# Attention ahead of two gated layers: the score, transpose and value stages one step further apart, and another order for the first steps

## The chip, the cores and the metric

The kernel runs on one core of one Trainium2 chip. The time is device microseconds for one execution of the whole program. Engines are named as the profile names them: PE (matrix multiply; PEld is its weight load), DVE (vector), ACT (scalar activation), POOL (GpSimd) and SP, which here only issues DMAs.

## The reference

Windowed causal attention feeds two dense layers in a row. All arrays are float32.

```
q, k, v: (4, 8, 576, 64)
scores = (q @ k^T) / 8 + slope_h * -|i - j|,  kept where 0 <= i - j < 128, else -1e9
attn   = softmax(scores) ;  a = attn @ v
x  = a as (2304, 512)                                  # tokens x (heads * 64)
x2 = (sigmoid(x @ w_gate) * (x @ w_val)) @ w_out        # 512 -> 1536 -> 512
h  = ((x2 @ w1) * (x2 @ w2)) @ w3                       # 512 -> 1024 -> 1024
out = h @ w_out2                                        # 1024 -> 512
```

## The kernel before

**Tiling.** The 2304 tokens are 18 tiles of 128, taken as five blocks of 2, 4, 4, 4 and 4 tiles (`TILES`). The 8 heads are four pairs; a pair fills 128 partitions. Attention is therefore 5 x 4 = 20 steps, step n being block n // 4 and pair n % 4 (`where`, `NSTEP`). The hidden width of the two layers is cut into slices of 128 that are taken two at a time (`groups`, `GF` = 2); a dense product is done in three float32r passes (high x high, high x low, low x high, `PASSES`), so every weight and every activation exists as a high and a low part.

**The three stages of an attention step.** `stage_s` (L418): PE computes the scores of up to four tiles and two heads into a PSUM tile that has a single buffer (`spsum`, tag `s`). For each two tiles DVE merges the two diagonals (L436), scales and adds the bias table (L439) and takes the negated row maximum (L445); for pairs other than the first ACT rescales that maximum (L449); ACT takes four exponentials with a row sum each (L452); DVE adds 1e-9 and inverts the sums (L455, L456); POOL multiplies each tile by its inverse (L459). `stage_p` (L461), for each of the two heads: PE transposes the tiles into a PSUM bank (L467), ACT copies it to `cp` (L470), POOL splits it by two selects into previous and own tile (L471, L475). `stage_pv` (L481): PE multiplies with v (L490), ACT and DVE write the high and low part of `xt` (L497, L498). Transposes, weighted values and the dense products below take their PSUM from one pool of four banks (`psmm`, tag `mm`).

**Fillers.** `layer(groups[0], blk)` is a generator for the first two slices of the first dense layer on one block: `gv` makes both gate products, then their sigmoids (ACT, L255), then the two value products, each followed by DVE's multiply (L260) and by the high and low parts `gt` (ACT, POOL); `down1` of the block before follows (L278). `fill(budget)` advances it by about that many ns of PE work. A layer for block b joins the list when the attention of that block is complete.

**The order.** PE's instructions run exactly in the order in which they are written (`manual_schedule`, L519). The other engines' and SP's order is laid down by a planner, which takes each instruction when it takes it to be ready, by priority; all queues are in order on the chip. Step n of the loop (L520) loads q and k for step n + 1 and v for step n + 1. For the first four steps it writes `stage_s(n)`, then `stage_p` and `stage_pv` of step n - 2; at step 4 scores, then both stages of steps 2 and 3, then the first filler; afterwards `stage_pv(n - 2)`, `stage_s(n)`, 600 ns of filler, `stage_p(n - 1)`, 3500 ns of filler.

**Weight conversion.** The weights arrive as float64 bit patterns. `convert_next` (L123) takes one from `queue`: ACT, five DVE instructions (L115 to L119) and POOL (L120) make a float32 (`rounded`), and ACT and POOL its two parts in `wsl`; or the float32 goes back to DRAM for a later stage. Twelve are taken during attention, at a priority 300 instructions later than their place: the six of the first group (`parts`, gate slices, then value slices, then output slices) and the six of the second, which are written to DRAM and fetched again once attention is over. The staging pool `conv0` is closed at step 15.

After attention the layers of all groups run over the blocks; nothing in the change touches that code.

Of the kernel before, what the change touches and what calls it, by code (L numbers as in the profile page):

```python
# [9 lines left out]
F32 = mybir.dt.float32  # L10
# [3 lines left out]
AF = mybir.ActivationFunctionType  # L14
ALU = mybir.AluOpType
# [4 lines left out]
P = 128  # L20

TILES = (2, 4, 4, 4, 4)
NBLK = len(TILES)
STARTS = tuple(sum(TILES[:i]) for i in range(NBLK))
TB = max(TILES) * P
# [4 lines left out]

PASSES = ((0, 0), (0, 1), (1, 0))
LATER = 300
FILL = (600.0, 3500.0)

FOLD_PLAN = ("cc", "ccccc", "cccfcfc", "cfcfcfcf", "cfcfcfcf")

# [8 lines left out]
def attn_moe_kernel(  # L45
# [14 lines left out]
    nc = tc.nc  # L60
# [77 lines left out]
    def convert_start(items):  # L138
        queue.extend(items)
        for it in queue[:2]:  # L140
            if it[0] not in staged:
                fetch(*it[:2])
# [10 lines left out]
            wsl[i] = wpools[par].tile([P, 3, 2, DM], F32R, name=f"wsl{i}", tag="w")  # L153
        return wsl[i][:, c, 0], wsl[i][:, c, 1]

    def parts(grp):
        def src(i, c):
            m = i - NF
            own = (w_gate, w_val, w_out)[c][i] if i < NF else (w1[m], w2[m], w3o[m * P : (m + 1) * P, :])[c]
            return ahead.get((i, c), own)  # L160

        return [((i, c), src(i, c), part_sink) for c in range(3) for i in grp]


    wo2 = {}
# [64 lines left out]
    def gv(grp, blk, xs, one):  # L230

        pss = {}
        w = cols(blk)
        ns = w / 2.4 + 13.3

        def product(i, s):
            full = gvpool.tile([P, TB], F32, tag=gvtag, name=f"gv{i}_{blk}_{s}", bufs=gvbufs)
            ps = pss[i, s] = full[:, 0:w]
            for kk in range(NK):
                for wp, xp in PASSES:  # L240
                    nc.tensor.matmul(  # L241
                        ps,
                        wsl[i][:, s, wp, kk * P : (kk + 1) * P],
                        xs[blk][:, xp, kk],
                        start=(kk == 0 and wp == 0 and xp == 0),
                        stop=(kk == NK - 1 and wp == 1),
                    )
                yield 3 * ns

        g = {}  # L250
        for i in grp:
            yield from product(i, 0)
        for i in grp:
            g[i] = m2.tile([P, TB], F32, tag="g", name=f"g{i}_{blk}")[:, 0:w]
            nc.scalar.activation(g[i], pss[i, 0], AF.Sigmoid if one else AF.Copy)  # L255
        ts = []
        for i in grp:
            yield from product(i, 1)
            pr = g[i]
            nc.vector.tensor_tensor(pr, pr, pss[i, 1], ALU.mult)  # L260
            t = m2.tile([P, 2, TB], F32R, tag="gt", name=f"gt{i}_{blk}", bufs=4)[:, :, 0:w]
            act_copy(t[:, 0], pr)
            pool_lo(t[:, 1], pr, t[:, 0])
            ts.append(t)
        return ts
# [61 lines left out]
    def attention(actx, conv):  # L327
# [9 lines left out]

        ident = cpool.tile([P, P], F32, name="ident")
        mask = cpool.tile([P, P], I32, name="mask")
        base = cpool.tile([P, 7, P], F32, name="base")  # L340

        PAIRS = {"nf": 0, "fn": 1, "nn": 2, "nc": 3, "ca": 4, "an": 5}
        KINDS = "fnnncannn" * 2
# [68 lines left out]

        def load_v(n):
            pair, blk, nt, t0, back = where(n)
            t = loads[n]["v"] = ap2.tile([P, 5, P], F32, tag="ldv", name=f"ldv{n}", bufs=4)
            nc.sync.dma_start(t[:, 1 - back : 1 + nt], v[pair, :, t0 - back : t0 + nt])

        def stage_s(n):  # L418
            pair, blk, nt, t0, back = where(n)
            s, ld = st[n], loads[n]  # L420
            x = s["sm"] = ap2.tile([P, 4, 2, P], F32, tag="sm", name=f"sm{n}", bufs=3)

            ps = spsum.tile([P, 4, 2, 2, P], F32, tag="s", name=f"s{n}")
            for t in range(nt):
                for h in range(2):
                    r = slice(D * h, D * h + D)
                    nc.tensor.matmul(  # L427
                        ps[:, t // 2 * 2 + h, :, t % 2], ld["q"][r, t * P : (t + 1) * P],
                        ld["k"][r, t * P : (t + 2) * P],
                        start=True, stop=True, skip_group_check=True,  # L430
                    )
            up = 4.0**pair
            for tp in range(nt // 2):
                g = slice(2 * tp, 2 * tp + 2)

                nc.vector.copy_predicated(  # L436
                    ps[:, g, 1], mask.unsqueeze(1).unsqueeze(1).broadcast_to([P, 2, 2, P]), ps[:, g, 0]
                )
                nc.vector.scalar_tensor_tensor(  # L439
                    x[:, g].rearrange("p g u k -> p g (u k)"), ps[:, g, 1].rearrange("p g u k -> p g (u k)"),  # L440
                    0.125 * up, tabs[blk][:, g].rearrange("p g u k -> p g (u k)"), ALU.mult, ALU.add,
                )
                mn = ap2.tile([P, 4], F32, tag="mn", name=f"mn{n}_{tp}", bufs=4)
                su = ap2.tile([P, 4], F32, tag="su", name=f"su{n}_{tp}", bufs=4)
                nc.vector.tensor_reduce(  # L445
                    mn, x[:, g].rearrange("p g u k -> p (g u) k"), axis=AX.X, op=ALU.max, negate=True
                )
                if pair:
                    nc.scalar.activation(mn, mn, AF.Copy, scale=1.0 / up)  # L449
                for j in range(4):  # L450
                    y = x[:, 2 * tp + j // 2, j % 2]
                    nc.scalar.activation(  # L452
                        y, y, AF.Exp, bias=mn[:, j : j + 1], scale=1.0 / up, accum_out=su[:, j : j + 1]
                    )
                nc.vector.tensor_scalar_add(su, su, 1e-9)  # L455
                nc.vector.reciprocal(su, su)  # L456
                for j in range(4):
                    y = x[:, 2 * tp + j // 2, j % 2]
                    nc.gpsimd.tensor_scalar(y, y, su[:, j : j + 1], 1.0, ALU.mult, ALU.mult)  # L459

        def stage_p(n):  # L461
            pair, blk, nt, t0, back = where(n)
            s = st[n]
            for h in range(2):
                ps = gvpool.tile([P, 4, P], F32, tag="mm", name=f"pt{n}_{h}")
                for t in range(nt):
                    nc.tensor.transpose(ps[:, t], s["sm"][:, t // 2 * 2 + h, t % 2], ident)  # L467
                cp = ap2.tile([P, 4, 2, P], F32, tag="cp", name=f"cp{n}_{h}")
                own, prev = cp[:, 0:nt, 1], cp[:, 0:nt, 0]
                act_copy(own, ps[:, 0:nt])  # L470
                nc.gpsimd.affine_select(  # L471
                    out=prev, in_=own, compare_op=ALU.is_gt, fill=0.0, base=0,
                    pattern=[[0, nt], [-1, P]], channel_multiplier=1,
                )
                nc.gpsimd.affine_select(  # L475
                    out=own, in_=own, compare_op=ALU.is_ge, fill=0.0, base=0,
                    pattern=[[0, nt], [1, P]], channel_multiplier=-1,
                )
                s["cp", h] = cp.rearrange("p t c k -> p (t c k)")
# [22 lines left out]
        def fill(budget):  # L502

            while fillers and budget > 0:
# [3 lines left out]
                else:  # L508
                    budget -= cost

        load(0)
        convert_start(parts(groups[0]) + second_items)
        load(1)
        load_v(0)
        consts()
        make_identity(nc, ident)
        table(0)
        HOT = NPAIR + 2
        with tc.manual_schedule(engines={mybir.EngineType.PE}):  # L519
            for n in range(NSTEP + 2):  # L520
                if 2 <= n + 1 < NSTEP:
                    load(n + 1)
                if 1 <= n + 1 < NSTEP:
                    load_v(n + 1)
                if n == 1:
                    consts2()
                if n % NPAIR == NPAIR - 2 and n // NPAIR + 1 < NBLK:
# [1 line left out]
                if n == 15:  # L529
# [2 lines left out]
                    accpools.append(  # L532
                        ctx.enter_context(tc.tile_pool(name="acc1", bufs=1, side="right", reuse_waits="tile"))
                    )
                if n < NPAIR:
                    stage_s(n)
                    if n >= 2:
                        stage_p(n - 2)
                        stage_pv(n - 2)
                elif n == NPAIR:  # L540
                    stage_s(n)
                    for m in (n - 2, n - 1):
                        stage_p(m)
                        stage_pv(m)
                    fillers.append(layer(groups[0], 0))
                    fill(FILL[1])
                else:
                    if n - 2 >= NPAIR:
                        stage_pv(n - 2)
                        if (n - 2) % NPAIR == NPAIR - 1 and (n - 2) // NPAIR < NBLK - 1:  # L550
                            fillers.append(layer(groups[0], (n - 2) // NPAIR))
                    if n < NSTEP:
                        stage_s(n)
                    fill(FILL[0])
                    if n - 1 < NSTEP:
                        stage_p(n - 1)
                    fill(FILL[1])
                if queue and (n < NPAIR + 2 or n % 2 == 0 or n > 9):
                    convert_next()
            while fillers:  # L560
                for _ in fillers.pop(0):
# [105 lines left out]
```

## Time and profile before

| | |
|---|---|
| Median of 3 runs | 977.85 us (977.38 to 977.97) |
| The profiled execution | 979.05 us; span 977.1 us |
| PE busy | 912.4 us (93%), 4528 matmuls |
| DVE, ACT, POOL busy | 581.1 us (59%), 338.6 us (35%), 329.0 us (34%) |
| Attention, by the PE order | scores from 4.2 us, last weighted values end at 235.9 us |
| Mean granted TensorE clock | 0.97 of 2.4 GHz |

The slices of the page show where PE is not busy and not at full clock (40 slices of 24.4 us):

```profile
PE   2487888989999899999999999999999999999998
DVE  6676565554698789689687247962862632431313
PEclk9686899899999999999999999999999999999999
```

Each digit is a tenth of a slice. The first ten slices are attention; in the other thirty PE is at nine nearly throughout.

### The profile page before, as it was taken

What the parts mean: (1) busy time and instruction counts of PE and PEld (TensorE: products, weight loads), DVE (VectorE), ACT (ScalarE), POOL (GpSimd) and SP (SyncE); (2) the same over time, 40 slices, a digit from 0 to 9 for tenths busy, and PEclk for the clock granted to TensorE, in tenths of its full rate; (3) what the DMA queues carried; (4) which work ended last, traced back from release to release, by engine and by line L of the source; (5) the groups of instructions that cost most, each with busy time, mean ns of one, the idle gap of its engine ahead of it and who ended that gap; (6) DMA issues with size and microseconds to landing.
All of it is one profiled execution on the core that took longest, in us unless ns stands there. A gap on an engine that the chain in (4) does not pass through costs nothing.

```text
span 977.1 us, 12272 instructions
## 1 busy us (share of the span) xinstructions
PE 912.4 (93%) x4528; PEld 744.3 (76%) x4528; DVE 581.1 (59%) x983; ACT 338.6 (35%) x784; POOL 329.0 (34%) x427
## 2 busy tenths in 40 slices
PE   2487888989999899999999999999999999999998
PEld 1264666667887788888888887888888888888887
DVE  6676565554698789689687247962862632431313
ACT  4364668474232242242232134343321311311110
POOL 5867565554332241231232111112431421421211
PEclk9686899899999999999999999999999999999999
DMA  5443332210433325114212022323330200000012
GB/s 168 158 151 127 111 93 84 76 39 27 147 108 118 108 74 160 58 67 157 68 65 97 1 76 92 113 78 108 107 98 1 85 24 1 21 1 1 33 54 107
DMA packets 32602, 79.68 MB, mean 82 GB/s; under 512 B 3616, under 2 KB 5664, under 8 KB 32544
## 3 DMA queue, kind: packets, MB, share of 16 engines
q1 hardware_dynamic: 32544, 78.92, 25.1%
q8 instruction: 35, 0.57, 0.3%
q14 instruction: 23, 0.19, 0.1%
HBM read 65.27 MB, written 13.63 MB: 81 GB/s over the span
## 4 chain that ended last, share of the span: by engine, by line
PE 78%; DVE 8%; ACT 6%; POOL 4%; DMA 3%; issue 1%; SPq 0%; ACTq 0%; DVEq 0%; POOLq 0%
PE gv L241 44%; PE dn L278 13%; PE o L302 10%; PE pv L490 4%; PE w3o L207 4%; ACT sm L452 2%; PE s L427 2%; POOL sm L459 1%; PE pt L467 1%; POOL cp L471 1%; ACT cp L68 1%; ACT L452 1%; POOL cp L475 1%; DMA raw_(0, 0)_94<-in_w_gate_dram 1%; ACT L255 1%
## 5 line engine op out<-in xcount | busy, mean ns | idle before, releaser
L241 PE MATMUL gv<-xt,wsl 128*128 128x512 f32 (+1 forms) x1440 | 310.0, 373 | 4.5 <-DVE g L260 3.2
L241 PEld LDWEIGHTS gv<-xt,wsl 128*128 128x128 f32 x1440 | 252.2, 191 | 53.2 <-DVE g L260 4.3
L74 POOL TENSOR_TENSOR gt<-g,gt 128x512 fp32r<-128x512 f32 (+1 forms) x100 | 120.0, 1203 | 422.0 <-ACT gt L68 421.8
L241 PE MATMUL gv<-x,wsl 128*128 128x512 f32 (+1 forms) x960 | 200.2, 368 | 0.0
L241 PEld LDWEIGHTS gv<-x,wsl 128*128 128x128 f32 x960 | 167.6, 189 | 30.1
L260 DVE TENSOR_TENSOR g<-g,gv 128x512 f32<-128x512 f32 (+1 forms) x100 | 62.6, 630 | 161.9 <-PE gv L241 161.9
L278 PE MATMUL dn<-gt,wsl 128*128 128x512 f32 (+1 forms) x720 | 153.6, 369 | 0.0
L278 PEld LDWEIGHTS dn<-gt,wsl 128*128 128x128 f32 x720 | 126.0, 189 | 23.0 <-issue 0.3
L68 ACT ACTIVATE gt<-g 128x512 fp32r<-128x512 f32 (+1 forms) x100 | 58.4, 587 | 143.9 <-DVE g L260 143.8
L255 ACT ACTIVATE g<-gv 128x512 f32<-128x512 f32 (+1 forms) x100 | 54.7, 549 | 152.5 <-PE gv L241 147.7
L302 PE MATMUL o<-wsl,gt 128*128 128x512 f32 x432 | 101.1, 389 | 0.0
L302 PEld LDWEIGHTS o<-wsl,gt 128*128 128x128 f32 x432 | 80.9, 188 | 16.6
L490 PE MATMUL pv<-cp,ldv 128*64 128x256 f32 (+1 forms) x352 | 57.1, 406 | 30.9 <-POOL cp L475 16.6
L490 PEld LDWEIGHTS pv<-cp,ldv 128*64 128x64 f32 x352 | 33.8, 160 | 54.6 <-POOL cp L475 24.8
L287 DVE TENSOR_TENSOR acc<-acc,dn 128x512 f32<-128x512 f32 (+1 forms) x100 | 62.3, 628 | 21.4 <-PE dn L278 20.9
L459 POOL TENSOR_SCALAR sm<-sm,su 128x128 f32<-128x128 f32 x144 | 56.4, 409 | 26.3 <-DVE su L456 19.2
L427 PE MATMUL s<-ldk,ldq 64*128 64x256 f32 x288 | 44.4, 453 | 16.3 <-DVE sm L439 6.2
L311 DVE TENSOR_TENSOR acc<-acc,o 128x512 f32<-128x512 f32 x54 | 37.1, 688 | 35.2 <-PE o L302 35.2
L452 ACT ACTIVATE sm<-sm,mn 128x128 f32<-128x128 f32 x144 | 55.9, 390 | 1.3 <-DVE mn L445 0.7
L427 PEld LDWEIGHTS s<-ldk,ldq 64*128 64x128 f32 x288 | 31.4, 224 | 25.0 <-issue 21.1
L207 PE MATMUL w3o<-wo,w3s 128*128 128x512 f32 x192 | 44.9, 391 | 0.7 <-DVE wo L71 0.5
L207 PEld LDWEIGHTS w3o<-wo,w3s 128*128 128x128 f32 x192 | 35.9, 188 | 9.1 <-DVE wo L71 0.8
(741 smaller groups left out, 861.7 us busy)
## 6 DMA issues: line engine op xcount, KB each, us to landing
ldk<-in_k_dram SPq DMA_DIRECT2D x16, 320.0 KB, 2.9
ldv<-in_v_dram SPq DMA_DIRECT2D x16, 320.0 KB, 2.8
out_dram<-acc SPq DMA_DIRECT2D x18, 256.0 KB, 2.0
ldq<-in_q_dram SPq DMA_DIRECT2D x16, 256.0 KB, 3.2
w3o<-w3os SPq DMA_DIRECT2D x8, 256.0 KB, 2.1
ldk<-in_k_dram SPq DMA_DIRECT2D x4, 128.0 KB, 3.3
ldq<-in_q_dram SPq DMA_DIRECT2D x4, 128.0 KB, 2.8
raw_(0, 0)_94<-in_w_gate_dram SPq DMA_DIRECT2D x1, 512.0 KB, 5.3
```

The costliest lines, as they stand in the source:

```text
L68: nc.scalar.activation(dst, src, AF.Copy)
L74: nc.gpsimd.tensor_tensor(dst, src, hi.bitcast(F32), ALU.subtract)
L207: nc.tensor.matmul(acc2, w3s[u][:, wp, i * P : (i + 1) * P], wo2[kk][:, xp], start=(kk == 0 and wp == 0 and xp == 0), stop=(kk == NC2 - 1 ...
L241: nc.tensor.matmul(ps, wsl[i][:, s, wp, kk * P : (kk + 1) * P], xs[blk][:, xp, kk], start=(kk == 0 and wp == 0 and xp == 0), stop=(kk == N ...
L255: nc.scalar.activation(g[i], pss[i, 0], AF.Sigmoid if one else AF.Copy)
L260: nc.vector.tensor_tensor(pr, pr, pss[i, 1], ALU.mult)
L278: nc.tensor.matmul(ps, wsl[i][:, 2, wp, m * P : (m + 1) * P], t[:, xp], start=n == 0, stop=n == 3 * len(grp) - 1,)
L302: nc.tensor.matmul(ps, t[:, xp, tt * P : (tt + 1) * P], wsl[i][:, 2, wp], start=n == 0, stop=n == 3 * len(grp) - 1,)
L427: nc.tensor.matmul(ps[:, t // 2 * 2 + h, :, t % 2], ld["q"][r, t * P : (t + 1) * P], ld["k"][r, t * P : (t + 2) * P], start=True, stop=Tru ...
L452: nc.scalar.activation(y, y, AF.Exp, bias=mn[:, j : j + 1], scale=1.0 / up, accum_out=su[:, j : j + 1])
L459: nc.gpsimd.tensor_scalar(y, y, su[:, j : j + 1], 1.0, ALU.mult, ALU.mult)
L490: nc.tensor.matmul(ps[c, a:b], loads[n]["v"][:, j + 1, c], s["cp", h][:, m0 : m0 + b - a], start=j == -back, stop=j == nt - 1, skip_group_ ...
```

## The change

The stages are set one step further apart: in step n the kernel writes `stage_p(n - 2)`, `stage_pv(n - 3)` and `stage_s(n)`, and then one call of `fill` of 4000 ns. Steps 0 to 6 have an order of their own (`ORDER`), and steps 5 to 9 their own filler budgets. v is loaded two steps later than before (`load_v(n - 1)`), with three buffers in place of four; `cp` has four in place of two. The twelve conversions are put to other steps (`CONVERT`); the first group's weights come gate and value slice by slice, and the first block's layer takes its sigmoid right after each gate product (`apart`). The rescaling of the maximum goes from ACT to DVE. The table `base` moves from a pool that lives through attention to the staging pool.

```diff
-FILL = (600.0, 3500.0)
+FILL = {5: 2800.0, 6: 0.0, 7: 1400.0, 8: 1400.0, 9: 1400.0}
+FULL = 4000.0
...
-    def parts(grp):
+    def parts(grp, apart=False):
...
+        keys = [(i, c) for c in range(3) for i in grp]
+        if apart:
+            keys = [(i, c) for i in grp for c in range(2)] + [(i, 2) for i in grp]
...
+        apart = blk == 0 and grp is groups[0]
...
         for i in grp:
+            if apart:
+                yield from product(i, 0)
+                g[i] = m2.tile([P, TB], F32, tag="g", name=f"g{i}_{blk}")[:, 0:w]
+                nc.scalar.activation(g[i], pss[i, 0], AF.Sigmoid)
             yield from product(i, 1)
...
-        base = cpool.tile([P, 7, P], F32, name="base")
+        base = spool.tile([P, 7, P], F32, name="base", bufs=1)
...
-            t = loads[n]["v"] = ap2.tile([P, 5, P], F32, tag="ldv", name=f"ldv{n}", bufs=4)
+            t = loads[n]["v"] = ap2.tile([P, 5, P], F32, tag="ldv", name=f"ldv{n}", bufs=3)
...
-                    nc.scalar.activation(mn, mn, AF.Copy, scale=1.0 / up)
+                    nc.vector.tensor_scalar(mn, mn, 1.0 / up, None, ALU.mult)
...
-                cp = ap2.tile([P, 4, 2, P], F32, tag="cp", name=f"cp{n}_{h}")
+                cp = ap2.tile([P, 4, 2, P], F32, tag="cp", name=f"cp{n}_{h}", bufs=4)
...
+        CONVERT = {0: 1, 2: 1, 4: 1, 6: 1, 8: 1, 9: 1, 10: 1, 11: 1, 12: 1, 13: 1, 14: 2}
+        ORDER = {
+            0: ((stage_s, 0),),
+            1: ((stage_s, 1),),
+            2: ((stage_s, 2), (stage_p, 0)),
+            3: ((stage_s, 3), (stage_pv, 0), (stage_p, 1)),
+            4: ((stage_s, 4), (stage_pv, 1), (stage_p, 2)),
+            5: ((stage_p, 3), (stage_pv, 2), (stage_s, 5), (stage_pv, 3)),
+            6: ((stage_p, 4), (stage_s, 6)),
+        }
...
-            for n in range(NSTEP + 2):
+            for n in range(NSTEP + 3):
...
-                if 1 <= n + 1 < NSTEP:
-                    load_v(n + 1)
+                if 0 <= n - 1 < NSTEP:
+                    load_v(n - 1)
...
+                for stage, m in ORDER.get(n, ((stage_p, n - 2), (stage_pv, n - 3), (stage_s, n))):
+                    if m < NSTEP:
+                        stage(m)
+                m = n - 3 if n > 7 else n - 2
+                if n >= 5 and m % NPAIR == NPAIR - 1 and m // NPAIR < NBLK - 1:
+                    fillers.append(layer(groups[0], m // NPAIR))
+                fill(FILL.get(n, FULL))
+                for _ in range(CONVERT.get(n, 0)):
                     convert_next()
```

## Rows read from the trace of the kernel before

**Rows 1.** Busy time by stretch: us, each engine (x instructions), clock, DMA share, GB/s
```profile
0.00:55.80 55.80, 23.73 (x96) 14.39 (x96) 34.61 (x65) 22.11 (x72) 36.83 (x66) 0.80 0.49 158
55.80:109.70 53.90, 41.20 (x227) 29.38 (x226) 40.27 (x77) 28.95 (x102) 38.72 (x68) 0.76 0.43 137
109.70:235.90 126.20, 115.24 (x737) 84.66 (x736) 70.18 (x140) 79.78 (x254) 69.71 (x148) 0.97 0.22 66
235.90:977.10 741.20, 732.26 (x3475) 615.88 (x3473) 436.01 (x701) 207.75 (x356) 183.70 (x146) 1.00 0.23 74
```

**Rows 2.** PE's longest waits in the first three stretches: us, times, longest
```profile
PE pv L490 <- POOL cp L475: 15.7, 6, 4.5
...
PE pt L467 <- POOL sm L459: 7.8, 5, 2.7
PE pv L490 <- POOL cp L471: 3.8, 8, 0.8
...
PE pv L490 <- POOL cp L471: 10.3, 7, 2.7
```

**Rows 3.** PE in order of time, one late attention step: start, us, instructions [idle before]
```profile
203.11 1.95 PE L490 MATMUL pv<-cp,ldv 128*64 128x128 f32 x20
204.99 2.00 PE L427 MATMUL s<-ldk,ldq 64*128 64x256 f32 x16
...
207.73 1.23 PE L467 MATMUL pt<-ident,sm 128*128 128x128 f32 x8
208.72 4.35 PE L241 MATMUL gv<-xt,wsl 128*128 128x512 f32 x18
...
216.17 2.43 PE L490 MATMUL pv<-cp,ldv 128*64 128x128 f32 x18 [2.74 <-POOL cp L471]
```

**Rows 4.** DVE's first instruction
```profile
8.21 0.43 DVE L115 TENSOR_SCALAR a_(0, 0)_147<-a_(0, 0)_147 128x512 f32<-128x512 f32 x1 [8.21 <-ACT a_(0, 0)_147 L114]
```

**Rows 5.** Busy time in two short early stretches (columns as in rows 1)
```profile
20.50:31.40 10.90, 5.29 (x22) 2.93 (x22) 8.70 (x16) 5.67 (x22) 9.64 (x14) 0.80 0.45 147
60.50:70.50 10.00, 8.55 (x65) 6.17 (x64) 9.39 (x16) 5.13 (x14) 8.27 (x12) 1.00 0.65 216
```

**Rows 6.** DVE, first and last of the last conversion's five instructions
```profile
98.36 0.42 DVE L115 TENSOR_SCALAR a_('ahead', 3, 2)_1408<-a_('ahead', 3, 2)_1408 128x512 f32<-128x512 f32 x1
...
100.46 0.69 DVE L119 SCALAR_TENSOR_TENSOR s_('ahead', 3, 2)_1409<-raw_('ahead', 3, 2)_1217,s_('ahead', 3, 2)_1409 128x512 f32<-128x512 uint32 x1
```

**Rows 7.** DVE groups, 0 to 109.7 us: busy us, mean ns of one, idle before
```profile
L456 DVE RECIPROCAL su<-su 128x4 f32<-128x4 f32 x14 | 2.4, 170 | 0.2
...
L117 DVE SCALAR_TENSOR_TENSOR a_(1, 0)_201<-raw_(1, 0)_96,a_(1, 0)_201 128x512 uint32<-128x512 uint32 x1 | 1.8, 1774 | 0.0
```

**Rows 8.** POOL's normalisation, 0 to 109.7 us and then 109.7 to 235.9 us
```profile
L459 POOL TENSOR_SCALAR sm<-sm,su 128x128 f32<-128x128 f32 x55 | 25.0, 472 | 1.9 <-DVE su L456 1.9
...
L459 POOL TENSOR_SCALAR sm<-sm,su 128x128 f32<-128x128 f32 x90 | 31.7, 371 | 24.4 <-DVE su L456 17.3 <-ACT cp L68 6.6 <-ACT sm L452 0.4
```

**Rows 9.** ACT in order of time: the copies of the transposes in two late steps
```profile
198.69 1.09 ACT L68 ACTIVATE cp<-pt 128x512 f32<-128x512 f32 x2 [2.66 <-PE pt L467]
...
209.91 0.58 ACT L68 ACTIVATE cp<-pt 128x512 f32<-128x512 f32 x1
210.51 1.28 ACT L452 ACT_TABLE_LOAD   x1
...
213.46 0.57 ACT L68 ACTIVATE cp<-pt 128x512 f32<-128x512 f32 x1
```

**Rows 10.** Every engine in order of time, the second group's weights after attention
```profile
235.97 0.33 SPq L102 DMA_DIRECT2D raw_(2, 0)_2123<-early  x1
...
247.45 1.29 POOL L74 TENSOR_TENSOR wsl<-raw_(3, 1)_2232,wsl 128x512 fp32r<-128x512 f32 x1 [0.18 <-ACT wsl L68]
...
250.73 5.92 PE L241 MATMUL gv<-xt,wsl 128*128 128x256 f32 x48
```

More of the change, by code (lines that the diff above doesn't have):

```diff
@@ L160, in src @@
             return ahead.get((i, c), own)
-        return [((i, c), src(i, c), part_sink) for c in range(3) for i in grp]
+        keys = [(i, c) for c in range(3) for i in grp]
+        if apart:
+            keys = [(i, c) for i in grp for c in range(2)] + [(i, 2) for i in grp]
+        return [(key, src(*key), part_sink) for key in keys]
     wo2 = {}
@@ L250, in gv @@
         g = {}
-        for i in grp:
+        apart = blk == 0 and grp is groups[0]
+        for i in () if apart else grp:
             yield from product(i, 0)
-        for i in grp:
+        for i in () if apart else grp:
             g[i] = m2.tile([P, TB], F32, tag="g", name=f"g{i}_{blk}")[:, 0:w]
@@ L509, in fill @@
                     budget -= cost
+        CONVERT = {0: 1, 2: 1, 4: 1, 6: 1, 8: 1, 9: 1, 10: 1, 11: 1, 12: 1, 13: 1, 14: 2}
[8 more added lines that the diff above has]
+        }
         load(0)
-        convert_start(parts(groups[0]) + second_items)
+        convert_start(parts(groups[0], apart=True) + second_items)
         load(1)
-        load_v(0)
         consts()
@@ L517, in attention @@
         table(0)
-        HOT = NPAIR + 2
         with tc.manual_schedule(engines={mybir.EngineType.PE}):
-            for n in range(NSTEP + 2):
+            for n in range(NSTEP + 3):
                 if 2 <= n + 1 < NSTEP:
                     load(n + 1)
-                if 1 <= n + 1 < NSTEP:
-                    load_v(n + 1)
+                if 0 <= n - 1 < NSTEP:
+                    load_v(n - 1)
                 if n == 1:
@@ L534, in attention @@
                     )
[L535 to L558, printed above, removed]
+                for stage, m in ORDER.get(n, ((stage_p, n - 2), (stage_pv, n - 3), (stage_s, n))):
[6 more added lines that the diff above has]
+                for _ in range(CONVERT.get(n, 0)):
                     convert_next()
```

## The prediction

> **What bounds the kernel now.** I read the busy time by stretch first, then PE's waits in each stretch, then PE in order of time, then the other engines where PE waits for them. The stretches are cut at PE's first filler (55.8 us), at the scores of step 9 (109.7 us) and at the end of the last weighted values (235.9 us). The last 741.2 us are PE's: it is busy for 732.3 of them at full clock, and nothing in the change touches that work [rows 1]. The 235.9 us before are three different things.
>
> To 55.8 us PE works 23.7 us and has no filler to run. Its largest wait is for the masked weights `cp`: 15.7 us in 6 waits, because weighted values come right behind the transposes of the same step [rows 1, 2]. DVE (34.6 us) and POOL (36.8 us) are the busiest engines. From 55.8 to 109.7 us PE is busy for 41.2 of 53.9 us, but at a mean clock of 0.76; DVE and POOL are busy for 40.3 and 38.7 us, and PE waits for POOL's normalisation (7.8 us) and selects (3.8 us) [rows 1, 2]. From 109.7 us fillers cover most: PE is busy for 115.2 of 126.2 us, and of its 11.0 us of idle time 10.3 are 7 waits for `cp`, three of them of some 2.7 us [rows 1 to 3]. So PE waits throughout on the chain of one step, and what stands behind that wait differs: in the first 110 us DVE and POOL are nearly full themselves, later they are half idle (70 of 126 us).
>
> **Part one, the waits for the chain.** After the change, between the transposes of step n and their weighted values, PE has the values of the step before (1.95 us), one set of scores (2.00), a filler (some 4.35 for 18 matmuls) and one set of transposes (1.23): 9.5 us. In the late step shown the transposes ended at 209.0 us and the second head's `cp` came at 216.2 us, 7.2 us later [rows 3]. 9.5 covers 7.2, so the wait for `cp` goes where a filler stands in the step. Transposes come two steps behind scores, at least 10 us of PE work where there are fillers; the wait there was no longer among the large ones before.
>
> **Part two, 109.7 to 235.9 us.** Three things go: 11.0 us of idle time; of the 126.2 us the clock's 3% (0.97), 3.8 us, since it falls where PE stops; and about 2 us that the three held-up value products take beyond their length (2.43 us for 18 where 20 take 1.95, so 0.7 each) [rows 1, 3]. That is 16.8 us. Two things come. The values of step 7, before, ended ahead of this stretch; now they lie in it: 1.95 us. And a new wait: the transposes take two of the four banks, then the values want one at once. Where a filler has broken off in the second gate product, the first still holds its bank until the sigmoids, and the second its own; the values must wait until ACT has copied the first transposes. With 6 quarter-products to a filler that is so in the second step of each of three layers, steps 11, 15 and 19. ACT's copy began with the end of the transposes in one step shown, and 0.95 us behind it in the other (209.91 against 208.96), and takes 0.6 us; the second head's copy came only at 213.5 us, behind a table load and four exponentials [rows 3, 9]. So a wait is between 0.4 and 5 us; I take 1.2 us, near the two first copies, and 3.6 us for three. The rest: 16.8 - 1.95 - 3.6 = 11.3 us gained, between 0 (three waits of 5 us) and 15.
>
> **Part three, 0 to 109.7 us.** Here PE stops being the measure: with the chain hidden, DVE or POOL decides. DVE's work is 34.6 + 40.3 = 74.9 us, POOL's 36.8 + 38.7 = 75.5 us [rows 1]. To DVE's work 11 rescalings of 128x4 values come (one each in steps 1 to 3, two each in 5, 6, 7 and 9); a reciprocal of that size takes 0.17 us [rows 7], so 1.9 us, 76.8 in all. One conversion costs DVE five instructions, 98.36 to 101.15 us less one inversion, some 2.7 us [rows 6]. Six of the twelve are now written at step 10 or later. But the one written at step 13 before ran at 98 us, in step 8: the planner draws them forward into gaps. I take it that three of six leave this stretch: 8.1 us, 68.7 left. DVE's first instruction is at 8.2 us, behind the first weights and ACT, and stays there [rows 4]. How full can DVE be? It reached 94% in one early stretch of 10 us and 80% in another, where POOL had 88% [rows 5]. At 87%, the middle: 8.2 + 68.7 / 0.87 = 87.2 us, where it was 109.7: 22.5 us gained. The ends: all six conversions gone and 94%, 8.2 + 60.6 / 0.94 = 73 us, 37 gained; none gone and 80%, 8.2 + 76.8 / 0.80 = 104 us, 6 gained. PE doesn't stand above this: what it did in 109.7 us was 64.9 us of work, part of it at half clock [rows 1].
>
> The banks decide nothing here, as fillers are short. Loads of v come two steps later, in SP's order behind those of q and k; with values three steps behind scores there are still two steps between a load and its use. Four buffers of `cp` hold two steps, which is what is under way at a time; three of `sm` and of `ldv` do too. The sigmoids set apart in the first block cost ACT one more change of tables each way, 2 x 1.28 us [rows 9]; ACT is busy for 29 of 53.9 us there [rows 1] and the rescaling leaves it. Cost on PE: none, or at most these 2.6 us if the normalisation of that step is late by it.
>
> A rule speaks against this part. In the trace a DVE instruction of the conversions took 1.77 us at a time when POOL ran a subtraction [rows 7], and POOL's normalisation took 0.472 us each in the first 110 us, against 0.371 later [rows 8]. The Trainium skill, page "SBUF — State Buffer", section "Who interferes with whom", says that DVE and GpSimd share a pair of ports under an exclusive lock, so that the later of two conflicting instructions blocks until the first is done. By it, work pressed into a shorter time overlaps more and each engine's busy time grows; that is the first rival.
>
> **Part four, what comes after.** The second group's weights are fetched when the last values are done (235.97 us), the last that the gate and value products need is ready at 248.7 us, and PE takes the first at 250.7 us [rows 10]. The chain hangs on the same event after the change, and PE has the same filler before it. I cost it at nothing; if a transfer comes late, some 5 us.
>
> **The sum.** The profiled execution took 979.05 us, 1.95 us more than its span. 979.05 - 22.5 - 11.3 = 945.3. That execution was 1.2 us above the median of the three runs, 977.85 us; the same 33.8 us off the median give 944.1. I predict 944 us.
>
> **The rivals.**
> First: the early stretch can't be pressed. DVE and POOL hold each other up; DVE's in-order queue, laid down by the planner, has an inversion waiting for ACT where scores could be merged. Then the early gain is the lower end, 6 us, with the 11 us later: 977.85 - 17 = 961. For it: POOL's 0.472 against 0.371 us [rows 8]. Against: 94% on DVE was seen with POOL at 83% [rows 5]. Chance 0.17.
> Second: better than the sum. The conversions do stay where they are written, the early end gains 30 to 37 us, and with 11 to 15 late the time is 925 to 937, or lower still. For it: the first five steps now have three conversions in place of five, and only 4 weights are wanted before step 8. Against: the one of step 13 seen in step 8. Chance 0.14.
> Third: it doesn't do what it says. The planner puts the later steps' work ahead of a step's normalisation on POOL and ACT, so what PE wants comes one step later too; the waits move and stay: 977. For it: POOL waits for ACT and for DVE in the late stretch, 24 us for the normalisation alone [rows 8], so order, not load, sets it there. Chance 0.04.
> Fourth, the other side: values wait for a bank in every full step, because the first copy comes as late as the second did (213.46 us, 4.5 us behind the transposes [rows 3, 9]). Twelve steps, 10 to 21, by 4.5 us and 0.6 for the copy itself make 61 us against 33.8: 1005 us. It decides from 33.8 / 12 = 2.8 us a step. For it: one queue on ACT holds both copies and eight exponentials. Against: only three steps find two banks taken. Chance 0.06.
>
> **How the numbers follow.** The forecast, both gains within a third of the sum, has 0.59: 935 to 957. The range to 0.8 takes in the first rival and half of the second: 924 to 966; the third and fourth and the end of the second are left out. Runs of this kernel differ by 0.06%; I count 0.2%, 2 us, as no change. Faster: forecast, first, second, and a little of the third and fourth, 0.91. Within 0.2%: 0.03, from the third. Slower: 0.06.
>
> **What would show it.** Right: PE's first filler near 40 us, the scores of step 9 near 87 us, the last values near 203 us, and the stretch behind it unchanged at 741 us. Waits of values for `cp` gone in steps 10 to 21, and three waits for ACT's copy. DVE above 80% busy to 87 us; where it isn't, and PE still waits, order and not load was the bound. The sum is wrong in part three if conversions sit late or DVE's instructions lengthen; in part two if PE waits for banks in more than three steps, or the clock is below 1.00 there; in part four if the stretch behind attention is not 741 us.

## The result, and the profile after

The changed kernel takes 947.3 us (median of 4 runs, 945.8 to 949.8) against 977.9 us (977.4 to 978.0) for the kernel before on the same chip: a ratio of 0.969 [0.967, 0.971]. 944 us was predicted, 924 to 966. The gain is 30.6 us where 33.8 were forecast. The profiled execution took 947.43 us, with a span of 945.7.

Busy time by stretch of the kernel after, cut at the same three places as [rows 1] (first filler, scores of step 9, end of the last weighted values); the columns are those of [rows 1]:

```profile
0.00:51.60 51.60, 24.75 (x113) 14.62 (x113) 34.83 (x71) 22.91 (x77) 38.47 (x70) 0.83 0.49 155
51.60:89.30 37.70, 26.85 (x192) 19.64 (x190) 31.34 (x67) 26.24 (x78) 31.99 (x54) 0.91 0.56 187
89.30:206.80 117.50, 112.11 (x751) 84.46 (x749) 77.30 (x173) 78.30 (x249) 78.23 (x159) 0.97 0.29 86
206.80:945.70 738.90, 732.38 (x3482) 617.03 (x3480) 432.03 (x701) 207.65 (x356) 183.98 (x146) 1.00 0.23 74
```

Against [rows 1] the four stretches gained 4.2, 16.2, 8.7 and 2.3 us, 31.4 in all. The first two, the early part, gained 20.4 (predicted 22.5); the late part 8.7 (predicted 11.3); the rest, which the prediction left at nothing, 2.3.

What PE waited for longest, in the second and then the third stretch of the kernel after (us, times, longest):

```profile
PE pt L476 <- POOL sm L468: 8.5, 5, 3.3
...
PE pt L476 <- POOL sm L468: 3.1, 4, 1.6
PE pv L499 <- issue: 1.3, 2, 0.7
PE pt L476 <- DVE g L269: 0.7, 1, 0.7
PE pv L499 <- POOL cp L484: 0.2, 1, 0.2
```

The 10.3 us of late waits for `cp` in [rows 2] are down to 0.2. A late step of the kernel after (start, us, instructions) shows why, beside [rows 3]:

```profile
180.13 1.04 PE L476 MATMUL pt<-ident,sm 128*128 128x128 f32 x8
181.09 1.95 PE L499 MATMUL pv<-cp,ldv 128*64 128x128 f32 x20
182.98 2.00 PE L436 MATMUL s<-ldk,ldq 64*128 64x256 f32 x16
184.90 4.40 PE L245 MATMUL gv<-xt,wsl 128*128 128x512 f32 x18
```

The values at 181.09 us use transposes of the step before; the step has no idle time in brackets and repeats every 9.0 us. In that step ACT copied the transposes of 180.13 us only at 185.31, behind eight exponentials (start, us):

```profile
182.21 0.40 ACT L461 ACTIVATE sm<-sm,mn 128x128 f32<-128x128 f32 x1
...
184.92 0.39 ACT L461 ACTIVATE sm<-sm,mn 128x128 f32<-128x128 f32 x1
...
185.31 1.06 ACT L69 ACTIVATE cp<-pt 128x512 f32<-128x512 f32 x2
```

A copy that comes 4.1 us after the transposes ended costs nothing here, since its values are due at about 190 us.

The third stretch is not even. Its first step is still an early one:

```profile
89.30:100.06 10.76, 8.06 (x47) 4.94 (x45) 8.86 (x20) 3.96 (x15) 9.98 (x16) 0.74 0.29 87
100.06:206.80 106.74, 104.05 (x707) 79.52 (x705) 68.44 (x153) 74.34 (x234) 68.25 (x144) 0.99 0.29 86
```

Step 9 took 10.8 us for 8.1 us of PE work at a clock of 0.74, with POOL busy for 9.98 of 10.76; the rest runs at 0.99.

### The profile page after: what moved, and what is told of

Read it like the earlier page. It is cut to its first block, busy times and chain, and to the rows that moved or that the text cites. A ratio compares the mean times of both kernels' runs of the same rounds, so it can differ in the third digit from the quotient of the medians.

```text
span 945.7 us, 12332 instructions
## 1 busy us (share of the span) xinstructions
PE 896.1 (95%) x4528; PEld 735.8 (78%) x4528; DVE 575.5 (61%) x1010; ACT 335.1 (35%) x759; POOL 332.7 (35%) x427
## 4 chain that ended last, share of the span: by engine, by line
PE 74%; DVE 8%; POOL 7%; ACT 5%; DMA 3%; issue 3%; SPq 0%; POOLq 0%; ACTq 0%; DVEq 0%
PE gv L245 43%; PE dn L287 12%; PE o L311 10%; PE w3o L211 5%; POOL sm L468 3%; ACT sm L461 2%; PE pv L499 2%; PE s L436 1%; POOL wsl L75 1%; POOL cp L484 1%; POOL cp L480 1%; PE pt L476 1%; ACT L461 1%; DMA early<-_('ahead', 'o2', 1)_2455 1%; DVE s L445 1%
## 5 line engine op out<-in xcount | busy, mean ns | idle before, releaser
L245 PE MATMUL gv<-xt,wsl 128*128 128x512 f32 (+1 forms) x1440 | 305.9, 371 | 4.3 <-DVE g L269 2.8
L468 POOL TENSOR_SCALAR sm<-sm,su 128x128 f32<-128x128 f32 x144 | 58.6, 426 | 32.5 <-DVE su L465 31.8
L436 PE MATMUL s<-ldk,ldq 64*128 64x256 f32 x288 | 41.7, 431 | 17.8 <-issue 7.7
L499 PE MATMUL pv<-cp,ldv 128*64 128x256 f32 (+1 forms) x352 | 43.3, 369 | 8.0 <-POOL cp L484 6.7
L499 PEld LDWEIGHTS pv<-cp,ldv 128*64 128x64 f32 x352 | 26.4, 148 | 23.9 <-POOL cp L484 10.9
```

The source lines that it names most:

```text
L245: nc.tensor.matmul(ps, wsl[i][:, s, wp, kk * P : (kk + 1) * P], xs[blk][:, xp, kk], start=(kk == 0 and wp == 0 and xp == 0), stop=(kk == N ...
L436: nc.tensor.matmul(ps[:, t // 2 * 2 + h, :, t % 2], ld["q"][r, t * P : (t + 1) * P], ld["k"][r, t * P : (t + 2) * P], start=True, stop=Tru ...
L499: nc.tensor.matmul(ps[c, a:b], loads[n]["v"][:, j + 1, c], s["cp", h][:, m0 : m0 + b - a], start=j == -back, stop=j == nt - 1, skip_group_ ...
```

## Experiments

The marks given for each are the first filler, the scores of step 9 and the end of the last values in its profiled run; after: 51.6, 89.3, 206.8. "Early", "late" and "rest" are the stretches they cut. Runs of the kernels close to the change differ by up to 0.5% among themselves, so 2 to 3 us between two of them are at the edge of what can be told; marks and stretches come from one profiled run each.

**The late part alone.** The order of before to step 9, the deeper one from step 10 on; rescaling stays on ACT.

```diff
-            for n in range(NSTEP + 2):
+            for n in range(NSTEP + 3):
...
+                elif n > 9:
+                    for stage, m in ((stage_p, n - 2), (stage_pv, n - 3), (stage_s, n)):
...
+                    fill(4000.0)
```

> The kernel before with its own order up to step 9, and the deeper order with one filler of 4000 ns from step 10 on (four cp buffers, three v buffers, base in the staging pool; conversions, sigmoids and the rescaling as before). Theory (two separate gains: hidden chain in the late steps, better packed DVE and POOL in the early ones): the scores of step 9 stay near 109.7 us, the stretch from there to the last values shrinks by some 9 to 11 us, time 967 to 970 us. Rival (one gain only, the early steps; the late stretch is PE's own work and what it saves is lost again in the stretch after): time within 2 us of 977.9 us.

Measured: 962.4 us (960.6 to 962.8), ratio 0.985 [0.982, 0.987]. Marks 55.6, 109.6, 224.7. Its late stretch and rest:

```profile
109.55:224.70 115.15, 108.08 (x730) 82.16 (x729) 70.94 (x140) 78.99 (x254) 69.06 (x147) 0.98 0.24 76
224.70:961.10 736.40, 731.26 (x3482) 615.69 (x3480) 431.80 (x701) 207.73 (x356) 183.66 (x146) 1.00 0.22 75
```

PE's waits of the values in that late stretch, the first and the last of five rows:

```profile
PE pv L490 <- ACT g L255: 3.5, 2, 2.2
...
PE pv L490 <- DVE g L260: 0.6, 1, 0.6
```

The late stretch fell by 11.05 us (126.2 to 115.15), `cp` is gone from the list, and the wait for a bank that the prediction added (3.6 us in three steps) is there: 4.1 us, in steps 11, 15 and 19 as named. The other three rows, 2.9 us, are waits of the transposes. The 11.3 us predicted are not this run's measure: here the values of step 7 still end ahead of the stretch, so the sum without their 1.95 us is 13.2. The profiled runs differ by 16.0 us (spans of 977.1 and 961.1); 4.8 of them came in the rest.

**The early part alone.** The kernel after to step 9, the order of before from step 10 on; rescaling stays on DVE.

```diff
+                else:
...
+                    fill(600.0)
...
+                    if n - 1 < NSTEP:
+                        stage_p(n - 1)
+                    fill(3500.0)
```

> The changed kernel up to step 9, and from step 10 on the order and the two fillers of the kernel before. Theory (the two gains are separate and add): with 15.4 of 30.6 us in the late steps, 15 us are left: 961 to 965 us, and the waits for cp of some 2.7 us come back in the late steps. Rival (the late steps gain only because the early ones end otherwise, or the reverse): below 955 us or above 970 us.

Measured: 973.6 us (971.5 to 975.3), 0.996 [0.995, 0.998]. The early part kept its gain (scores of step 9 at 89.6), but the late stretch grew from 126.2 to 143.3 us:

```profile
89.60:232.90 143.30, 123.63 (x757) 87.45 (x755) 79.14 (x173) 77.43 (x247) 78.86 (x159) 0.93 0.23 71
```

PE's longest waits in it:

```profile
PE pv L499 <- POOL cp L480: 12.1, 5, 4.7
PE pt L476 <- POOL sm L468: 5.8, 8, 2.5
PE pv L499 <- POOL cp L484: 1.6, 3, 0.7
```

So the two halves do not add: 14.6 and 3.8 us alone, 30.6 together. The old late order comes out worse than it did in the kernel before: its longest waits for `cp`, three of 2.74 us before (one is in [rows 3]), are here 2.0, 4.3 and 4.7, the first of them in step 10, where the two orders meet. ACT in order of time, around the second of them:

```profile
152.76 0.60 ACT L69 ACTIVATE cp<-pt 128x512 f32<-128x512 f32 x1
154.23 1.28 ACT L461 ACT_TABLE_LOAD   x1 [0.87 <-DVE mn L458]
155.53 0.41 ACT L461 ACTIVATE sm<-sm,mn 128x128 f32<-128x128 f32 x1
...
158.24 0.39 ACT L461 ACTIVATE sm<-sm,mn 128x128 f32<-128x128 f32 x1
...
158.63 0.58 ACT L69 ACTIVATE cp<-pt 128x512 f32<-128x512 f32 x1
```

Between the two heads' copies stand a table load, a wait for the rescaled maximum and all eight exponentials: 5.9 us. In the kernel before the copies of that place were 3.55 us apart [rows 9], with four exponentials between them and an ACT rescaling of the second two tiles (0.19 us at 213.36) just ahead of the second copy.

**The rescaling alone.** The kernel before with only this edit; its PE order is unchanged.

```diff
-                    nc.scalar.activation(mn, mn, AF.Copy, scale=1.0 / up)
+                    nc.vector.tensor_scalar(mn, mn, 1.0 / up, None, ALU.mult)
```

> The kernel before with one edit: the rescaling of the maximum on DVE. Theory (the kernel with only the early steps changed lost 17 us in the late ones because the old order has no slack, so that any other planner order lengthens its waits for cp): late stretch longer than 126.2 us by 4 us or more, waits for cp of 3 us or more each, time 981 us or more. Rival (the edit is free in either order, and the loss there has another cause): time within 3 us of 977.5 us.

Measured: 985.7 us (983.6 to 987.5), 1.009 [1.007, 1.011]: slower. Scores of step 9 at 102.6, last values at 243.4:

```profile
102.55:243.40 140.85, 121.65 (x737) 86.26 (x737) 74.33 (x160) 79.17 (x245) 70.72 (x150) 0.92 0.19 60
```

PE in order of time, the three long waits of it [idle before]:

```profile
126.20 1.12 PE L490 MATMUL pv<-cp,ldv 128*64 128x128 f32 x4 [4.67 <-POOL cp L471]
...
171.50 0.86 PE L490 MATMUL pv<-cp,ldv 128*64 128x128 f32 x4 [4.64 <-POOL cp L471]
...
220.23 1.12 PE L490 MATMUL pv<-cp,ldv 128*64 128x128 f32 x4 [4.68 <-POOL cp L471]
```

It won 7.1 us early and lost 14.6 late: the same 737 matmuls have 19.2 us of idle time where they had 11.0 and, at a clock of 0.92 instead of 0.97, 6.4 us more of busy time. The three waits, before at the same steps 2.74 us each, are now 4.7; in the last of them the two copies stand at 210.94 and 217.43 with the eight exponentials between them. An edit of 0.2 us an instruction thus lengthens the chain by changing where the planner puts a copy in ACT's queue, and a pipeline of the old depth pays for it.

**The rescaling back on ACT**, in the kernel after: the diff above, reversed.

> The changed kernel with the rescaling of the maximum back on ACT. Theory (it is a side edit; ACT has room): within 3 us of the changed kernel's 947 us. Rival (the hop to ACT, behind ACT's in-order queue of copies and exponentials, is what held the chain): slower by 6 us or more, most of it before the scores of step 9.

Measured: 951.1 us (948.6 to 952.7), 0.974 [0.971, 0.976]; marks 51.2, 92.0, 210.3. At most 4 us, with intervals that just meet: in the deeper pipeline the edit is worth a little or nothing, where it cost the old one about 9. What it saves there can be seen: with the rescaling back on ACT, the three waits for a bank stand in steps 11, 15 and 19 again, as in the late part alone:

```profile
PE pv L499 <- ACT g L260: 4.8, 3, 2.1
```

**The first block's sigmoids not set apart**, and the gate slices' weights first again.

```diff
-        apart = blk == 0 and grp is groups[0]
+        apart = False
```

> The changed kernel without the sigmoids set apart: weights come gate slices first, and the first block's layer makes both gate products before its sigmoids. Theory (all four slices were there by 41 us, the filler began at 51.6 us): within 3 us of 947 us. Rival (the order of the slices lets the filler begin earlier): slower by 5 us or more, first filler later than 55 us.

Measured: 948.3 us (947.9 to 949.0), 0.971 [0.969, 0.973]; first filler at 52.5, scores of step 9 at 90.2: no difference that can be told.

**The first block's sigmoids left out.** `Copy` in place of the sigmoid, which is not computed there, so that ACT need not change tables.

```diff
-                nc.scalar.activation(g[i], pss[i, 0], AF.Sigmoid)
+                nc.scalar.activation(g[i], pss[i, 0], AF.Copy)
```

> The changed kernel, leaving out the sigmoid of the first block's two gate slices of the first group (a copy in its place, which needs no change of ACT's table). Theory (with half of the conversion load away the early steps still took 33.6 us, so ACT's in-order queue with its table changes is the other limit there): from the first filler to the scores of step 9 33 to 35 us in place of 37.7, time 942 to 945 us. Rival (the order on DVE and POOL alone): stretch within 1 us of 37.7, time 946 us or more.

Measured: 948.4 us (946.5 to 950.2), 0.972 [0.969, 0.974]; scores of step 9 at 91.4. The four table loads of 1.28 us that stood between the first filler and the scores of step 9 are gone, and nothing is won.

**The own order left out**: the first steps take the general order, and the first filler is written in step 6 in place of 5.

```diff
-                for stage, m in ORDER.get(n, ((stage_p, n - 2), (stage_pv, n - 3), (stage_s, n))):
+                for stage, m in ((stage_p, n - 2), (stage_pv, n - 3), (stage_s, n)):
```

> The changed kernel without the own order of steps 0 to 6: transposes two and values three steps behind from the start, first filler of 2800 ns in step 6. Theory (the first steps are held by POOL and DVE, so PE's order there matters little): 945 to 950 us, first filler within 3 us of 51.6 us or made good by step 9. Rival (the own order is what brings the first filler forward): slower by 5 us or more than 947 us.

Measured: 949.8 us (947.9 to 951.3), 0.973 [0.970, 0.975]; marks 67.6, 93.5, 211.3. The first filler comes 16 us later, the scores of step 9 only 4.2, and the time is 2.5 us longer: when the fillers begin hardly matters, since the stretch behind then runs faster.

**The conversions at the old places.**

```diff
-        CONVERT = {0: 1, 2: 1, 4: 1, 6: 1, 8: 1, 9: 1, 10: 1, 11: 1, 12: 1, 13: 1, 14: 2}
+        CONVERT = {0: 1, 1: 1, 2: 1, 3: 1, 4: 1, 5: 1, 6: 1, 8: 1, 10: 1, 11: 1, 12: 1, 13: 1}
```

> The changed kernel with the twelve conversions written at the steps where the kernel before had them (0 to 6, 8, 10 to 13). Theory (the planner draws conversions forward into gaps wherever they are written): within 3 us of 947 us, the last conversion ending near 103 us as now. Rival (their places are a part of the early gain): slower by 5 us or more, scores of step 9 later than 94 us.

Measured: 944.1 us (943.4 to 945.4), 0.967 [0.965, 0.969]; marks 52.9, 87.0, 206.1. If anything 3 us better. Writing the conversions later did not move them later.

**Half of the conversions without arithmetic.** The second group's six conversions keep ACT's pass and the transfers, and leave out DVE's five instructions and POOL's sum.

```diff
+    def bare(t, key):
...
+        nc.scalar.activation(x, t[:, :, 1].bitcast(F32), AF.Abs)
+        return x
```

> The changed kernel, leaving out DVE's and POOL's arithmetic in the conversion of the second group's six weights (ACT's one pass and the transfers stay). Theory (once the chain is hidden, DVE's and POOL's load decides the early steps: four and a half conversions lie ahead of the scores of step 9, 2.7 us of DVE each): scores of step 9 at 76 to 81 us in place of 89.3, time 933 to 940 us. Rival (order and latency of the chain decide, not load): scores of step 9 at 86 us or later, time above 943 us.

Measured: 939.1 us (937.8 to 939.6), 0.962 [0.959, 0.965]; marks 52.1, 85.7, 198.9.

```profile
52.10:85.70 33.60, 28.38 (x190) 22.11 (x188) 20.65 (x49) 26.18 (x80) 23.59 (x52) 0.85 0.65 221
85.70:198.90 113.20, 108.23 (x750) 82.74 (x749) 72.87 (x161) 78.12 (x246) 71.92 (x155) 1.00 0.27 85
```

The total fell as the load theory said (8.2 us), but only 3.6 of it ahead of step 9's scores, where 8 to 13 were expected; 4.3 came in the late stretch. With DVE 10.7 and POOL 8.4 us emptier the second stretch shrank by 4.1.

**The second group's conversions later, by their fetches.** The planner draws a conversion forward as soon as its weights lie ready, so here each fetch is held behind the load of a step; first in steps 9 to 14 with the conversions in 11 to 16, then in steps 13 to 18 with the conversions in 14 to 19. The first group's output slices are fetched in steps 6 and 7 in both.

```diff
+                if n in FETCH:
+                    with tc.issue_after(getattr(last_load[0], "ins", last_load[0])):
+                        fetch(*items[FETCH[n]][:2])
```

> The changed kernel with conversions really held back: the fetch of the first group's output slices and of the second group's six weights is issued behind the q load of steps 6, 7 and 9 to 14, so that no conversion can be drawn forward past it; staging pool closed at step 18. Theory (early steps bound by DVE and POOL load, late steps with room on both): scores of step 9 at 74 to 80 us, the late stretch longer by 0 to 3 us, time 935 to 941 us, better than both kernels. Rival (order, not load; or the conversions collide with the late steps): scores of step 9 at 86 us or later, time 945 us or more.

> As the kernel with conversions held back, but the second group's six are fetched in steps 13 to 18 and converted from step 14 on, one a step, beside full fillers; staging pool closed at step 20. Theory (held back to steps 11 to 13 they met the end of a layer and a step with little filler; from step 14 on DVE and POOL are busy for under two thirds and PE has 9 us a step): scores of step 9 at 82 to 84 us, steps 10 to 13 without the 15.5 us step, last values at 197 to 202 us, time 937 to 942 us, better than both kernels. Rival (a conversion costs the attention some 1.3 us wherever it stands, since it delays what is queued behind it on DVE and POOL): 946 us or more.

Measured: 949.2 us (947.7 to 950.3), 0.972 [0.969, 0.974], and 945.2 us (944.6 to 945.6), 0.968 [0.966, 0.969]. The first run's late stretch:

```profile
83.30:208.80 125.50, 113.23 (x751) 85.80 (x749) 92.01 (x192) 81.70 (x252) 85.32 (x161) 0.96 0.34 110
```

and the second's:

```profile
82.10:205.60 123.50, 113.05 (x751) 84.00 (x749) 89.58 (x192) 81.47 (x252) 85.05 (x161) 0.99 0.36 116
```

Early they win 6.0 and 7.2 us, late they lose 8.0 and 6.0. The first has a single wait of 4.57 us for DVE's gate product in step 12. Both missed the hope of 935 to 942. It looks as if a conversion costs its time wherever it stands, but the second run lies between that rival (946 or more) and the theory.

**Both of these together**, the early and the later places: the first group's conversions in steps 0 to 5, the second group's in 14 to 19. The edit is shown against the second of the two runs above.

```diff
-        CONVERT = {0: 1, 2: 1, 4: 1, 5: 1, 8: 1, 9: 1, 14: 1, 15: 1, 16: 1, 17: 1, 18: 1, 19: 1}
+        CONVERT = {0: 1, 1: 1, 2: 1, 3: 1, 4: 1, 5: 1, 14: 1, 15: 1, 16: 1, 17: 1, 18: 1, 19: 1}
```

> The kernel after, with the second group's six weights fetched from step 13 and converted in steps 14 to 19 (as in the run that put these conversions later), and the first group's six converted one a step in steps 0 to 5, fetched as in the kernel after. Theory (the light steps are held by several things together, and conversions cost some 1 to 2 us each wherever they stand): early conversions in the first five steps cost little there, the first filler comes near 48 us, the scores of step 9 near 81, the late stretch takes 123 us as with the later conversions, the rest 737: 941 to 946 us, so 0 to 6 us below the kernel after (947.3). Rival (the two gains, 3 us from the earlier places and 2 us from the later conversions, are run scatter and have no cause): 946 to 950 us. Second rival (the two add up without loss in the late stretch): 938 to 941.

Measured: 946.8 us (942.6 to 947.5), 0.967 [0.964, 0.969]; marks 51.0, 82.0, 206.8. The late stretch takes 124.8 us and returns what the early part won. The run with the old places stays the best of those that compute the same, 3 us below the change, where the runs of one kernel scatter by up to 5.

## Why the prediction was right, and where it was not

**Part one and two, the chain and the late stretch: right by the mechanism named, with terms off in size.** The waits for `cp` are gone, alone and in the kernel after. Alone the late order gains 11.05 us where 13.2 were due, in the kernel after 8.7 where 11.3 were due. In both the transposes wait, which the prediction put at nothing: 2.9 us alone, 3.8 in the kernel after, 2.6 of these in step 9, which still behaves like an early step (10.76 us at a clock of 0.74). And the 3.8 us taken for the clock did not come back there: the stretch as a whole stands at 0.97 as before, at 0.99 only behind step 9.

The three waits for a bank are right for another kernel than the one predicted. They come in steps 11, 15 and 19 where the rescaling is on ACT (4.1 us in the late part alone, 4.8 with the rescaling put back), and in none of these steps of the kernel after. There ACT takes the first gate slice's sigmoid in time: in step 14 at 143.48 us, ahead of all eight exponentials, and the values written in step 15 follow at 144.27 without a wait. In the late part alone, with the rescaling on ACT, the sigmoid of that place stands behind four exponentials, at 160.55, and the values follow it at 161.20. The prediction took both sigmoids to come after the second gate product. What the kernel after has instead are two short waits of the values in steps 13 and 17, which I read, without a run that shows it, as waits for a bank:

```profile
128.62 1.95 PE L499 MATMUL pv<-cp,ldv 128*64 128x128 f32 x20 [0.54 <-issue]
...
163.10 1.95 PE L499 MATMUL pv<-cp,ldv 128*64 128x128 f32 x20 [0.74 <-issue]
```

With the 0.7 us for DVE's gate product, just ahead of the first, that makes 2.0 us where 3.6 were taken. The fourth rival (values wait for a bank in every full step, as the copy comes late) fell: the copy does come 4.1 us late in the step shown, and the values behind those transposes don't wait.

**Part three, the early part: the size right, its reason half right.** "DVE or POOL decides" held in part, and more for POOL than for DVE, with which I computed. DVE was busy for 66.2 us up to step 9's scores (34.83 + 31.34), from 7.2 us on 81% and not 87. In the second stretch POOL is the fullest engine, 32.0 of 37.7 us (85%, DVE 83%), where it had 38.7 of 53.9 before [rows 1]. The chain of that stretch, by line, shares of its length (the last entry of the row is cut off):

```profile
by line: POOL sm L468 28.5%; POOL cp L484 11.7%; issue 9.8%; POOL cp L480 7.9%; ACT sm L461 7.2%; POOL tab L409 4.0%; POOL a_('ahead', 2, 1)_1221 L121 3.8%; ACT L266 3.4%; ACT L461 3.4%; POOL wsl L75 3.3%; POOL a_('ahead', 3, 0)_1094 L121 3
```

The six POOL lines given in full make 59%: normalisation, selects, a table, a conversion's sum and a split, one behind the other in one queue. That is what PE's 8.5 us for `sm` are. Where POOL and DVE are relieved, the next limit stands close by. In the last run above, with POOL busy for 22.5 of 31.0 us, the same chain reads:

```profile
by line: PE pv L499 17.8%; POOL sm L468 14.8%; PE s L436 13.7%; PE pt L476 8.2%; POOL cp L480 7.9%; PE gv L245 6.3%; ACT sm L461 5.2%; DVE s L445 4.2%; ACT L461 4.1%; POOL a_(1, 2)_517 L121 4.0%; POOL cp L484 4.0%; DVE sm L448 2.3%; DVE mn 
```

PE leads it, with some 27 us of work in the stretch at a clock of 0.89. So the load of DVE and POOL explains 3.6 to 7 us ahead of step 9's scores, and the runs got no more by taking it away or moving it; the best of them gained 27.7 us early against the kernel before (109.7 to 82.0), short of the second rival's 30 to 37. Where the 20.4 us come from is not shown piece by piece. The rescaling alone brought 7.1 early in the old order, a gain for which the working has no term. Taken out of the kernel after, it costs 2.7 early, the sigmoids set apart 0.9 and the own order 4.2. The greater stage distance of the early steps, by itself, was not run.

Three steps of the working failed. "Three of six leave this stretch": four of the second group's six conversions were done before step 9's scores, since the planner draws them forward whatever step they are written at (the run with the old places shows that it doesn't matter). The "first filler near 40 us" came at 51.6. And the 1.9 us for eleven rescalings, by the price of a reciprocal, were too few: up to step 9's scores nine of them took twice that:

```profile
L458 DVE TENSOR_SCALAR mn<-mn 128x4 f32<-128x4 f32 x9 | 3.8, 422 | 0.0
```

DVE's work was still 2.5 us less than the 68.7 taken and began 1.0 us earlier, but DVE was less full; these partly cancelled, and the sum came out 2.1 us off. That the size came so near is in part luck.

The first rival said that DVE and POOL hold each other up. A sign of it is there: POOL's normalisation takes 465 ns each in the second stretch and 379 from 100 us on, as in [rows 8], and one DVE instruction of a conversion took 1.77 us again, as in [rows 7]. In the run without the second group's arithmetic the same stretch has 375 ns. First the kernel after, then that run:

```profile
L468 POOL TENSOR_SCALAR sm<-sm,su 128x128 f32<-128x128 f32 x28 | 12.5, 465 | 2.9 <-DVE su L465 2.9
...
L473 POOL TENSOR_SCALAR sm<-sm,su 128x128 f32<-128x128 f32 x29 | 10.3, 375 | 6.6 <-PE s L441 3.6 <-DVE su L470 3.1
```

So it is the conversions beside them that lengthen POOL's instructions, by some 2.5 us in that stretch (28 of 90 ns), not by the 16 of that rival. This agrees with the lock that the Trainium skill, page "SBUF — State Buffer", section "Who interferes with whom", describes.

**Part four, "nothing": off by 2.3 us.** The rest took 741.2 us before and 738.9 after. The difference is in PE's waits there: 5.1 us in six before (3.2 for DVE's gate product, 1.2 for ACT's sigmoid, 0.7 later for `wo`), 2.8 in one after, for the gate product. Why they differ is open. With the old late order the rest takes 738.4 to 741.2 us in three runs, with the deeper one 736.4 to 738.9 in eleven, so the depth may have a part in it; nothing was tried for this stretch alone.

**What the prediction didn't see** is that its parts hang together. It costed the rescaling as 1.9 us of DVE work. In the old pipeline that edit costs 9 us in all, 14.6 in the late stretch through ACT's order. The deeper pipeline is worth more than the waits that it removes from the kernel before: in it, where the planner puts a copy matters less (the rescaling is worth at most 4 us there). That is, as I read the runs, how 14.6 and 3.8 make 30.6: of the 17.1 us by which the early part alone lengthened the late stretch, 1.95 are the values of step 7, which now lie in it, and the rescaling alone lengthened it by 14.6. The early part with the rescaling on ACT, ahead of the old late order, was not run.

## What to carry to other kernels

Where PE's order is written by hand and the other engines' by a planner, a pipeline that just covers the chain of one step can pay dearly for a rearrangement: here an edit of 0.2 us an instruction moved a copy behind eight exponentials. One step more depth costs buffers and a wait or two for banks, and it should be put in before other edits are judged, because what they are worth can depend on it. Measure halves of a change alone before adding them up.

## What was not expected of the hardware

Waits cost PE twice. The 20 value products of a step took 1.95 us in a late step and 3.68 at 96.44 us in the kernel after, behind waits of 0.4, 0.5 and 1.6 us for `sm`, in a step whose granted clock was 0.74: the lower of the two levels (1.2 GHz of 2.4) for part of it. In the run with only the rescaling 8.2 us more of idle time came with 6.4 us more of busy time for the same matmuls.

Changes of ACT's tables, 1.28 us each, were free in the early part: taking four away gained nothing. ACT is busy there for 26 of 37.7 us.
